# A spectral-filter and gated-MLP kernel: the first three gated units made one row tile at a time, seven units in the first pass, two projections at the end

## The chip, the cores and the metric

The kernel runs on one core of a Trainium2 chip. The metric is the device time of one execution in microseconds (us), as the median of several runs. The core has a matrix engine (PE, with its weight loads shown apart as PEld), a vector engine (DVE), a scalar engine (ACT), a general engine (POOL) and a queue that issues most DMAs (SP; ACT can issue DMAs too). Each engine takes its own instructions in program order and waits on semaphores for the others.

## The reference: what is computed

The input `x` has 2048 rows of 512 bf16 numbers. It is normalized by rows, and two branches are added to it:

```python
xn = _layernorm(x, axis=-1)
return x + _A_ref(xn, A_w_r, A_w_i) + _B_ref(xn, B_w_gate, B_w_up, B_w_down)

# branch A: a filter in the frequency domain, W = w_r + 1j * w_i
irfft2(rfft2(xn) * W)
# branch B: a gated MLP, 512 -> 1792 -> 512
h = gelu(xn @ w_gate) * (xn @ w_up)
h @ w_down
```

## The kernel before, in words

The 2048 rows are 16 row tiles of 128 rows (`NJ`), and four of them are a block of 512 rows (`b` from 0 to 3). The 1792 hidden columns are 14 chunks of 128 (`fc`).

**Branch B.** For a block, the normalized rows `xn` are transposed to `xnT` (four chunks of 128 of the 512 columns lie on the partitions). `geglu_unit(b, fc, a, w)` (L529) makes one chunk of the hidden layer for `w` rows from row `a` of the block: four gate matmuls into one PSUM bank, four up matmuls into the next (L543), a gelu of the gate bank on ACT into `gg` (L555), and a product of the up bank and `gg` on DVE into `hT` (L563). Its PSUM banks come from a ring; a bank is taken again when its reader (the gelu or the product) is done. Such a unit is called a gated unit here. `down_unit(b, jj)` (L577), a projection, makes one row tile of the output: 14 matmuls (L589) and an addition into `x_sb` on DVE (L600).

**Branch A** is a 2-D Fourier filter as small matmuls (L616, L642, L691, L722, L753, L774), with shuffles through DRAM between its stages: A and d for each row tile, then B, a product and c for each of 16 pairs, then e and fin for each row tile. The first stage needs the normalized rows folded: POOL makes half folds (L504) of four tiles at a time, DVE mirror folds (L509). `unit_fin` (L765) ends the branch for one row tile: ACT and DVE unpack the bank (L781, L784, L785), DVE and POOL make two halves (L788), POOL adds them into `x_sb` (L792). The later of this and the projection's addition issues the row tile's output DMA on SP (L575).

**The order is written out by hand** (L798 to L909). A recording layer keeps a list for each engine in the order in which the Python calls come, and puts a wait for every dependency that the engine has not waited for yet. So whatever stands earlier in a list holds back all that stands behind it on that engine. The order is:

1. Loads. ACT issues the identity and columns 0 to 383 of `w_up` (chunks 0 to 2); SP issues row tiles 0 and 1 of `x`, the same columns of `w_gate`, row tiles 2 and 3, then the other weight pieces and rows (L343 to L375). Each piece has one semaphore for both matrices.
2. Row tiles 0 and 1: statistics on DVE (`ln_stats`, L411 and L412), the root of both on ACT (L417), the reciprocal of both on DVE (L421), and the normalization of each on DVE (`ln_apply`, L434). Meanwhile PE runs 46 small warm-up matmuls on zeros, and 4 more that wait for the reciprocal (`NWARM`, L524). ACT loads the gelu's table and runs it once on one column (L802).
3. `transposes_by_tile(0, 2)` (L439): PE transposes both tiles into four banks (L447), one for each column chunk; DVE and ACT copy two banks each to `xnT` (L453, L455).
4. The statistics of tiles 2 and 3 on DVE, and their reciprocal root on POOL (`ln_rstd`, L426 and L427).
5. The first pass: block 0's gated units of chunks 0 to 5 (`NHALF` is 6) for the 256 rows of tiles 0 and 1, with a ring of six banks. After chunk 1 tiles 2 and 3 are normalized and POOL folds tiles 0 to 3; after chunk 3 tiles 2 and 3 are transposed (`transposes`, L473, copied at L480 and L482).
6. The same six units for tiles 2 and 3.
7. What is left of branch B is a list of fillers, in order: eight units of block 0, then units and projections of the later blocks (each block's four projections stand among the next block's units), and block 3's four projections at the end. Branch A's stages run one after another, and a filler is put between two of their steps: one filler before each A step (`j` from 0 to 15), some around the shuffles, one in each of 17 B and c steps (`u`), then all but 18 of those that are left, 15 between the e and fin steps, and the last 3 behind the last fin step. So a filler that is taken out of the list at its head moves all others one place forward.

Of the kernel before, what the change touches and what calls it, by code (L numbers as in the profile page):

```python
# [14 lines left out]
HD = 256  # L15
NK = 257
FF = 1792
P = 128
NJ = 16
NG = 32  # L20
NDC = 4
# [3 lines left out]
NWARM = (46, 4)  # L25
# [126 lines left out]
class _Sched:  # L152
# [14 lines left out]
    def total(self, stream):  # L167
        return (stream, self.stream_cnt[stream])
# [59 lines left out]
def bass_parallel_sum__spectral_gfnet__glu_gated_geglu__prompt_kernel(  # L228
# [21 lines left out]
    with ExitStack() as es:  # L250
# [68 lines left out]
        def sp_bank_bf(slot):  # L319
# [10 lines left out]
        streams = [("pe", 1), ("act", 1), ("dve", 1), ("pool", 1)]  # L330
        streams += [(n, 16) for n in ("x0", "x1", "x2", "x3", "xc1", "xc2", "xc3", "ident", "small", "fa", "eg", "wd", "wr", "wi",
                                      "w0", "w1", "w2", "w3", "w4", "dr0", "dr1", "perm1", "jx0", "jx1", "jx2", "jx3", "vd0_0", "vd0_1", "vd0_2", "vd1_0", "vd1_1", "vd1_2", "vd2_0", "vd2_1", "vd2_2", "vd3_0", "vd3_1", "vd3_2", "perm2", "tr2", "tr3", "out")]
# [106 lines left out]
        def transposes_by_tile(a, b, ring):  # L439

            n = (b - a) * P
            slots = [ring.alloc(1) for _ in range(NDC)]
            banks = [sp_bank_bf(slot)[:, 0:n] for slot, _ in slots]
            evs = []
            for j in range(a, b):
                for r in range(NDC):
                    ev_t = sch.op("pe", lambda e, j=j, r=r: e.transpose(banks[r][:, (j - a) * P:(j - a + 1) * P], xn[:, j, r * P:(r + 1) * P], ident),  # L447
                                  deps=[ev_id, ev_xn[j]] + slots[r][1])
                    if j < b - 1:
                        continue  # L450
                    dst = xnT[:, r, a * P:b * P]
                    if r % 2 == 0:
                        ev = sch.op("dve", lambda e, dst=dst, r=r: e.tensor_copy(dst, banks[r]), deps=[ev_t])  # L453
                    else:
                        ev = sch.op("act", lambda e, dst=dst, r=r: e.activation(dst, banks[r], ACT.Copy), deps=[ev_t])  # L455
# [73 lines left out]
        def geglu_unit(b, fc, a=0, w=512, ring=None):  # L529
# [6 lines left out]
            evw = [ev_w[i] for i, (lo, hi) in enumerate(WPIECES) if lo < (fc + 1) * P and fc * P < hi]  # L536
# [16 lines left out]
            ev_um = sch.op("pe", lambda e: mm(e, wu_sb, uslot), deps=udeps)  # L553
# [244 lines left out]
        NHALF = 6  # L798
        ln_stats(0)
        ln_stats(1)  # L800
        ev_sq = ln_sqrt(0, 2)
        sch.op("act", lambda e: e.activation(warm[:], eps_t[:], ACT.Gelu_apprx_tanh), deps=[ev_eps])  # L802
# [97 lines left out]
        filler(todo["left"] - 15 - 3)  # L900
# [59 lines left out]
```

## Time and profile before

| what | us |
|---|---|
| median of 3 runs | 180.47 (180.36 to 180.71) |
| profiled execution, its own time | 180.17 |
| its span in the trace | 178.4 |
| PE busy in the span | 174.7 |
| DVE busy | 116.0 |
| ACT busy | 86.5 |
| POOL busy | 55.2 |
| PE's first gated matmul starts | 7.14 |

The table is read so: the profiled execution is one run, 0.30 us under the median, and its span leaves out 1.8 us around the program. An engine's busy time is the sum of the time in which it has an instruction under way. In a timeline's line the first number is the start in us from the span's start, the second the time to the end of the last instruction of the group, then engine, source line, operation, what is written and read, shape and count; the bracket tells how long the engine was idle before and who ended it. PE's instructions overlap: the next starts before the one before has ended, so its pace is read from starts.

### The profile page before, as it was taken

What the parts mean: (1) busy time and instruction counts of PE and PEld (TensorE: products, weight loads), DVE (VectorE), ACT (ScalarE), POOL (GpSimd) and SP (SyncE); (2) the same over time, 40 slices, a digit from 0 to 9 for tenths busy, and PEclk for the clock granted to TensorE, in tenths of its full rate; (3) what the DMA queues carried; (4) which work ended last, traced back from release to release, by engine and by line L of the source; (5) the groups of instructions that cost most, each with busy time, mean ns of one, the idle gap of its engine ahead of it and who ended that gap; (6) DMA issues with size and microseconds to landing.
All of it is one profiled execution on the core that took longest, in us unless ns stands there. A gap on an engine that the chain in (4) does not pass through costs nothing.

```text
span 178.4 us, 3133 instructions
## 1 busy us (share of the span) xinstructions
PE 174.7 (98%) x1136; PEld 98.2 (55%) x1136; DVE 116.0 (65%) x250; ACT 86.5 (49%) x159; POOL 55.2 (31%) x54
## 2 busy tenths in 40 slices
PE   7999999999999999999999999999999999999994
PEld 7888465555555544454555555444455555555443
DVE  3768958798685628438586785954355868885731
ACT  2644357777362633066375764632173536662100
POOL 0073290373630000000000000000017869997760
PEclk9999999999999999999999999999999999999999
DMA  4999999999998693913435666744500111111101
GB/s 147 323 342 379 372 379 149 202 156 239 221 159 198 150 313 106 324 53 81 123 104 125 123 184 149 177 90 117 118 6 29 59 59 32 61 65 48 41 29 59
DMA packets 37520, 27.15 MB, mean 152 GB/s; under 512 B 6656, under 2 KB 36736, under 8 KB 37376
## 3 DMA queue, kind: packets, MB, share of 16 engines
q1 hardware_dynamic: 33664, 24.95, 55.1%
q10 hardware_dynamic: 3840, 2.00, 5.8%
q8 instruction: 9, 0.15, 0.4%
q14 instruction: 7, 0.06, 0.2%
HBM read 17.48 MB, written 6.30 MB: 133 GB/s over the span
## 4 chain that ended last, share of the span: by engine, by line
PE 87%; POOL 5%; DVE 5%; issue 1%
PE ps L543 48%; PE ps L589 25%; POOL bufC L504 5%; PE ps L524 3%; PE ps L722 2%; PE ps L753 2%; PE ps L774 2%; PE ps L691 2%; DVE bufA L434 2%; DVE hT L563 1%; PE ps L616 1%; PE ps L642 1%; PE ps L473 1%; DVE bufB L509 1%; POOL rstd L427 1%
## 5 line engine op out<-in xcount | busy, mean ns | idle before, releaser
L543 PE MATMUL ps<-xnT,wg_sb 128*128 128x512 bf16 (+1 forms) x248 | 58.5, 359 | 0.3 <-DVE xnT L453 0.3
L543 PE MATMUL ps<-xnT,wu_sb 128*128 128x512 bf16 (+1 forms) x248 | 58.6, 359 | 0.0
L563 DVE TENSOR_TENSOR hT<-ps,gg 128x512 bf16<-128x512 f32 (+1 forms) x62 | 39.3, 637 | 23.2 <-PE ps L543 21.6
L589 PE MATMUL ps<-wd_sb,hT 128*128 128x512 bf16 (+2 forms) x238 | 50.7, 367 | 0.0
L555 ACT ACTIVATE gg<-ps 128x512 bf16<-128x512 f32 (+1 forms) x62 | 34.4, 555 | 25.2 <-PE ps L543 23.6
L788 POOL TENSOR_TENSOR bufC<-bufC 128x256 bf16<-128x256 f32 x16 | 14.7, 919 | 86.5 <-DVE bufC L785 86.5
L543 PEld LDWEIGHTS ps<-xnT,wu_sb 128*128 128x128 bf16 x248 | 24.2, 98 | 24.2
L589 PEld LDWEIGHTS ps<-wd_sb,hT 128*128 128x128 bf16 x238 | 22.4, 98 | 23.2
L543 PEld LDWEIGHTS ps<-xnT,wg_sb 128*128 128x128 bf16 x248 | 23.0, 98 | 15.4 <-issue 0.5
L600 DVE TENSOR_TENSOR x_sb<-ps,x_sb 128x512 bf16<-128x512 f32 (+2 forms) x17 | 11.2, 660 | 23.9 <-PE ps L589 23.9
L792 POOL TENSOR_TENSOR x_sb<-x_sb,bufC 128x512 bf16<-128x512 bf16 x16 | 18.7, 1169 | 2.3
L504 POOL TENSOR_TENSOR bufC<-bufA 128x1024 bf16<-128x1024 bf16 x8 | 16.8, 2124 | 7.9 <-DVE bufA L434 7.9
L758 ACT ACTIVATE bufA<-ps 128x512 bf16<-128x512 f32 x16 | 9.4, 597 | 16.9 <-PE ps L753 16.9
L727 ACT ACTIVATE Vp<-ps 128x514 bf16<-128x514 f32 x16 | 9.5, 599 | 15.4 <-PE ps L722 15.4
L650 ACT ACTIVATE bufB<-ps 128x512 bf16<-128x512 f32 x16 | 11.9, 743 | 9.5 <-PE ps L642 9.5
L411 DVE BATCH_NORM_STATS2 st<-x_sb 128x6 f32<-128x512 bf16 x16 | 10.9, 678 | 2.2 <-DMA x_sb<-in_A_x_dram 2.2
L784 DVE TENSOR_TENSOR bufC<-bufC,ps 128x256 f32<-128x256 f32 x16 | 6.7, 421 | 5.3 <-ACT bufC L781 5.3
L696 ACT ACTIVATE Xc<-ps 128x514 bf16<-128x514 f32 x12 | 7.0, 595 | 1.0 <-PE ps L691 1.0
L623 ACT ACTIVATE tmp<-ps 128x512 bf16<-128x512 f32 x9 | 5.4, 597 | 4.4 <-PE ps L616 4.4
L426 POOL TENSOR_SCALAR rstd<-ag 128x4 f32<-128x4 f32 (+1 forms) x4 | 1.3, 316 | 19.9 <-DVE ag L412 19.9
L781 ACT ACTIVATE bufC<-ps 128x256 f32<-128x256 f32 x16 | 6.0, 378 | 2.6 <-PE ps L774 2.6
L788 DVE TENSOR_TENSOR bufC<-bufC 128x256 bf16<-128x256 f32 x16 | 6.8, 425 | 0.5
(50 smaller groups left out, 138.0 us busy)
## 6 DMA issues: line engine op xcount, KB each, us to landing
stage_g<-Vp SPq DMA_DIRECT2D x16, 128.5 KB, 3.1
bufC<-stage_p SPq DMA_DIRECT2D x4, 512.0 KB, 5.5
out_dram<-x_sb SPq DMA_DIRECT2D x15, 128.0 KB, 1.8
wd_sb<-in_B_w_down_dram SPq DMA_DIRECT2D x1, 1792.0 KB, 14.8
stage_p<-bufB SPq DMA_DIRECT2D x7, 256.0 KB, 5.6
wr_sb<-in_A_w_r_dram SPq DMA_DIRECT2D x6, 257.0 KB, 10.8
wi_sb<-in_A_w_i_dram SPq DMA_DIRECT2D x6, 257.0 KB, 10.0
JX<-Xc SPq DMA_DIRECT2D x24, 64.2 KB, 2.3
```

Of the source, the lines that this page charges most:

```text
L411: ev = sch.op("dve", lambda e: e.bn_stats(st[:, j, :], x_sb[:, j, :]), deps=[ev_x[j]])
L504: ev_hf[m] = [sch.op("pool", lambda e, t=t, op=op: e.tensor_tensor(half[:, m, t, :, :], rows[:, 0, :, :], rows[:, 1, :, :], op), deps=deps ...
L543: ins = e.matmul(gu_bank(slot)[:, 0:w], wsb[:, dc, fc * P:(fc + 1) * P], xnT[:, dc, b * 512 + a:b * 512 + a + w], start=(dc == 0), stop=(d ...
L555: ev_gg = sch.op("act", lambda e: e.activation(gg, gu_bank(gslot)[:, 0:w], ACT.Gelu_apprx_tanh), deps=[ev_gm] + gg_readers[s2])
L563: ev_h = sch.op("dve", lambda e: e.tensor_tensor(hT[hb][:, fc, a:a + w], gu_bank(uslot)[:, 0:w], gg, ALU.mult), deps=[ev_um, ev_gg] + hdeps)
L589: ins = e.matmul(bank(slot)[:, 0:w], hT[hb][:, fc, jj * P:(jj + 1) * P], wd_sb[:, fc, cs], start=(fc == 0), stop=(fc == NFC - 1))
L600: ev_a = sch.op("dve", lambda e, slot=slot, cs=cs, w=w: e.tensor_tensor(x_sb[:, j, cs], bank(slot)[:, 0:w], x_sb[:, j, cs], ALU.add), deps ...
L650: ev_T[j] = sch.op("act", lambda e: e.activation(dst, src, ACT.Copy), deps=[ev_p])
L727: ev_v = sch.op("act", lambda e: e.activation(Vp[sv][:], sp_pair(slot), ACT.Copy), deps=[ev_p] + Vp_readers[sv])
L758: ev_ZT[j] = sch.op("act", lambda e: e.activation(ZT[:, :, j, :], src, ACT.Copy), deps=[ev_p] + [ev_xnT[i][0] for i in (11, 15)])
L788: y = [sch.op(("dve", "pool")[h], lambda e, h=h, op=op: e.tensor_tensor(rS[s2][:, h * HD:(h + 1) * HD], yeS[s2][:, 0, :], yeS[s2][:, 1, :] ...
L792: ev_o = sch.op("pool", lambda e: e.tensor_tensor(x_sb[:, j, :], x_sb[:, j, :], rS[s2], ALU.add), deps=[a, b, ev_xn[j]] + ev_acc.get(j, []))
```

## The change

- **Loads.** SP issues row tiles 0 and 1, then columns 0 to 383 of `w_gate` and of `w_up`, then row tiles 2 and 3. ACT issues the identity alone. Gate and up pieces have semaphores of their own, and a unit's up matmuls wait for the up piece.
- **Tiles 0 and 1 apart.** The root is taken and inverted for each of the two tiles by itself. On DVE the order is: reciprocal 0, normalization 0, reciprocal 1, the two copies of tile 0's transposes, normalization 1. `transpose_first` transposes one tile into two banks of `ring_tr`, two column chunks in each, and copies them on DVE (tile 0) or ACT (tile 1). Tile 1's transposes stand behind tile 0's first unit.
- **Three units for one tile at a time.** Chunks 0 to 2 are made for the 128 rows of tile 0, then for those of tile 1. The statistics of tile 2 stand behind tile 0's units, those of tile 3 behind tile 1's first unit.
- **First pass of seven.** Chunks 3 to 6 follow for 256 rows; tiles 2 and 3 are normalized after chunk 3 and transposed after chunk 5. Then seven units for tiles 2 and 3. The list of fillers begins with seven units of block 0, so it is one shorter.
- **Warm-up** matmuls are 42 and 3, where they were 46 and 4.
- **The end.** 17 fillers are kept back for the e and fin steps and behind them, where it was 18: 15 as before, and 2 behind the last fin step.

```diff
@@ -22,7 +22,7 @@
 NFC = 14
 NGG = 3
 NX1 = 4
-NWARM = (46, 4)
+NWARM = (42, 3)
 LN_EPS = 1e-5
 
 
@@ -328,8 +328,9 @@
         ring_tr = _Ring((3, 4), bank_readers)
 
         streams = [("pe", 1), ("act", 1), ("dve", 1), ("pool", 1)]
+        streams += [("w%d%s" % (i, q), 16) for i in range(5) for q in "gu"]
 ...
-                                      "w0", "w1", "w2", "w3", "w4", "dr0", "dr1", ...)]
+                                      "dr0", "dr1", ...)]
         for name, inc in streams:
             sem = es.enter_context(nc.semaphore("sem_" + name))
             sch.add_stream(name, sem, inc)
@@ -349,8 +350,9 @@
             a, b = WPIECES[i]
             for q in which:
                 dst, src = ((wg_sb, B_w_gate), (wu_sb, B_w_up))[q]
-                load("w%d" % i, dst[:, :, a:b], src[:, a:b].rearrange("(r p) f -> p r f", p=P), eng=eng)
-            ev_w[i] = total("w%d" % i)
+                name = "w%d%s" % (i, "gu"[q])
+                load(name, dst[:, :, a:b], src[:, a:b].rearrange("(r p) f -> p r f", p=P), eng=eng)
+                ev_w[i, q] = total(name)
 
         def load_xc(m):
             ev = load("xc%d" % m, x_sb[:, 4 * m:4 * m + 4, :], xv[:, 4 * m:4 * m + 4, :])
@@ -358,11 +360,11 @@
                 ev_x[j] = ev
 
         ev_x = {}
-        load_w(0, (1,), eng="act")
-        for j in range(4):
+        for j in (0, 1):
             ev_x[j] = load("x%d" % j, x_sb[:, j, :], xv[:, j, :])
-            if j == 1:
-                load_w(0, (0,))
+        load_w(0)
+        for j in (2, 3):
+            ev_x[j] = load("x%d" % j, x_sb[:, j, :], xv[:, j, :])
         load_w(1)
         load_w(2)
         load_xc(1)
@@ -436,27 +438,28 @@
 
         ev_xnT = {}
 
-        def transposes_by_tile(a, b, ring):
-
-            n = (b - a) * P
-            slots = [ring.alloc(1) for _ in range(NDC)]
-            banks = [sp_bank_bf(slot)[:, 0:n] for slot, _ in slots]
+        def transpose_first(j, eng):
+
             evs = []
-            for j in range(a, b):
-                for r in range(NDC):
-                    ev_t = sch.op("pe", lambda e, j=j, r=r: e.transpose(banks[r][:, (j - a) * P:(j - a + 1) * P], xn[:, j, r * P:(r + 1) * P], ident),
-                                  deps=[ev_id, ev_xn[j]] + slots[r][1])
-                    if j < b - 1:
-                        continue
-                    dst = xnT[:, r, a * P:b * P]
-                    if r % 2 == 0:
-                        ev = sch.op("dve", lambda e, dst=dst, r=r: e.tensor_copy(dst, banks[r]), deps=[ev_t])
-                    else:
-                        ev = sch.op("act", lambda e, dst=dst, r=r: e.activation(dst, banks[r], ACT.Copy), deps=[ev_t])
-                    ring.add_reader(slots[r][0], ev)
-                    evs.append(ev)
-            for j in range(a, b):
-                ev_xnT[j] = evs
+            for h in range(2):
+                slot, bdeps = ring_tr.alloc(1)
+                bank = sp_bank_bf(slot)[:, 0:HD].rearrange("p (r s) -> p r s", r=2)
+
+                def f_tr(e, h=h, bank=bank):
+                    ins = None
+                    for r in range(2):
+                        ins = e.transpose(bank[:, r, :], xn[:, j, (2 * h + r) * P:(2 * h + r + 1) * P], ident)
+                    return ins
+
+                ev_t = sch.op("pe", f_tr, deps=[ev_id, ev_xn[j]] + bdeps)
+                dst, src = xnT[:, 2 * h:2 * h + 2, j * P:(j + 1) * P], bank
+                if eng == "dve":
+                    ev = sch.op("dve", lambda e, dst=dst, src=src: e.tensor_copy(dst, src), deps=[ev_t])
+                else:
+                    ev = sch.op("act", lambda e, dst=dst, src=src: e.activation(dst, src, ACT.Copy), deps=[ev_t])
+                ring_tr.add_reader(slot, ev)
+                evs += [ev, ev]
+            ev_xnT[j] = evs
 
         def transposes(a, b, ring, per=2):
 
@@ -533,7 +536,8 @@
             s2 = k % NGG
             hb = b % 2
             ring = ring or ring_gu
-            evw = [ev_w[i] for i, (lo, hi) in enumerate(WPIECES) if lo < (fc + 1) * P and fc * P < hi]
+            pieces = [i for i, (lo, hi) in enumerate(WPIECES) if lo < (fc + 1) * P and fc * P < hi]
+            evw, evw_up = ([ev_w[i, q] for i in pieces] for q in range(2))
             evx = [ev_xnT[4 * b + i] for i in range(a // P, (a + w) // P)]
             gslot, gdeps = ring.alloc(1)
 
@@ -550,7 +554,7 @@
             else:
                 ev_gm = sch.op("pe", lambda e: mm(e, wg_sb, gslot), deps=evw + evx + gdeps)
             uslot, udeps = ring.alloc(1)
-            ev_um = sch.op("pe", lambda e: mm(e, wu_sb, uslot), deps=udeps)
+            ev_um = sch.op("pe", lambda e: mm(e, wu_sb, uslot), deps=evw_up + udeps)
             gg = gg_sb[s2][:, 0:w]
             ev_gg = sch.op("act", lambda e: e.activation(gg, gu_bank(gslot)[:, 0:w], ACT.Gelu_apprx_tanh),
                            deps=[ev_gm] + gg_readers[s2])
@@ -795,27 +799,35 @@
             finished(j, ev_o)
 
 
-        NHALF = 6
+        NQUARTER, NHALF = 3, 7
         ln_stats(0)
         ln_stats(1)
-        ev_sq = ln_sqrt(0, 2)
+        ev_sq = [ln_sqrt(j, j + 1) for j in range(2)]
         sch.op("act", lambda e: e.activation(warm[:], eps_t[:], ACT.Gelu_apprx_tanh), deps=[ev_eps])
-        ln_recip(0, 2, ev_sq)
+        ln_recip(0, 1, ev_sq[0])
         for n, ev in zip(NWARM, (None, ev_rstd[0])):
             warm_up(n, ev)
         ln_apply(0)
+        ln_recip(1, 2, ev_sq[1])
+        transpose_first(0, "dve")
         ln_apply(1)
-        transposes_by_tile(0, 2, ring_sp)
+        for fc in range(NQUARTER):
+            geglu_unit(0, fc, 0, P, ring_first)
+            if fc == 0:
+                transpose_first(1, "act")
         ln_stats(2)
-        ln_stats(3)
+        for fc in range(NQUARTER):
+            geglu_unit(0, fc, P, P, ring_first)
+            if fc == 0:
+                ln_stats(3)
         ln_rstd(2, 4)
-        for fc in range(NHALF):
+        for fc in range(NQUARTER, NHALF):
             geglu_unit(0, fc, 0, 256, ring_first)
-            if fc == 1:
+            if fc == NQUARTER:
                 ln_apply(2)
                 ln_apply(3)
                 half_fold(0)
-            if fc == 3:
+            if fc == NHALF - 2:
                 transposes(2, 4, ring_tr)
         for fc in range(NHALF):
             geglu_unit(0, fc, 256, 256, ring_first)
@@ -897,7 +909,7 @@
                 back(u // 4 - 2, (u - 9) % 4, "act")
         for pq in range(2):
             back(3, pq, "sp")
-        filler(todo["left"] - 15 - 3)
+        filler(todo["left"] - 15 - 2)
         for j in range(NJ + 2):
             if j < NJ:
                 unit_e(j)
```

More of the change, by code (lines that the diff above doesn't have):

```diff
@@ L330, in bass_parallel_sum__spectral_gfnet__glu_gated_geglu__prompt_kernel @@
         streams = [("pe", 1), ("act", 1), ("dve", 1), ("pool", 1)]
+        streams += [("w%d%s" % (i, q), 16) for i in range(5) for q in "gu"]
         streams += [(n, 16) for n in ("x0", "x1", "x2", "x3", "xc1", "xc2", "xc3", "ident", "small", "fa", "eg", "wd", "wr", "wi",
-                                      "w0", "w1", "w2", "w3", "w4", "dr0", "dr1", "perm1", "jx0", "jx1", "jx2", "jx3", "vd0_0", "vd0_1", "vd0_2", "vd1_0", "vd1_1", "vd1_2", "vd2_0", "vd2_1", "vd2_2", "vd3_0", "vd3_1", "vd3_2", "perm2", "tr2", "tr3", "out")]
+                                      "dr0", "dr1", "perm1", "jx0", "jx1", "jx2", "jx3", "vd0_0", "vd0_1", "vd0_2", "vd1_0", "vd1_1", "vd1_2", "vd2_0", "vd2_1", "vd2_2", "vd3_0", "vd3_1", "vd3_2", "perm2", "tr2", "tr3", "out")]
         for name, inc in streams:
```

## The prediction

> **What bounds the kernel now.** I read the page first, then the timeline of the first 30 us, then the chain of waits and the timeline at the places where the chain leaves PE.
>
> ```profile
> span 178.4 us, 3133 instructions
> PE 174.7 (98%) x1136; PEld 98.2 (55%) x1136; DVE 116.0 (65%) x250; ACT 86.5 (49%) x159; POOL 55.2 (31%) x54
> PE 87%; POOL 5%; DVE 5%; issue 1%
> ```
>
> PE is never long without work. So the change can gain only in the head (before PE's first gated matmul), in small PE waits, and in the tail after PE's last matmul. The matmuls stay the same in sum: only their cut into columns changes.
>
> The head, from the timeline (start, time to the group's end, engine, line):
>
> ```profile
> 0.97 5.41 PE L524 MATMUL ps<-hT 128*128 128x128 bf16 x50 [0.97 <-DVE hT L405]
> ...
> 4.67 0.18 DVE L412 BATCH_NORM_AGGREGATE ag<-st 128x2 f32<-128x6 f32 x1
> ...
> 5.20 1.28 ACT L802 ACT_TABLE_LOAD   x1
> ...
> 5.42 0.73 DVE L434 TENSOR_SCALAR bufA<-x_sb,ag,rstd 128x512 bf16<-128x512 bf16 x2
> ...
> 6.22 0.61 PE L447 MATMUL ps<-small,bufA 128*128 128x128 bf16 x8
> ...
> 6.70 0.49 DVE L453 COPY xnT<-ps 128x256 bf16<-128x256 bf16 x2 [0.55 <-PE ps L447]
> 6.76 0.66 ACT L455 ACTIVATE xnT<-ps 128x256 bf16<-128x256 bf16 x2
> ...
> 7.14 0.62 PE L543 MATMUL ps<-xnT,wg_sb 128*128 128x256 bf16 x4 [0.31 <-DVE xnT L453]
> ...
> 7.93 0.66 DVE L411 BATCH_NORM_STATS2 st<-x_sb 128x6 f32<-128x512 bf16 x1
> ...
> 9.20 0.73 POOL L427 TENSOR_TENSOR rstd<-rstd,half_t 128x2 f32<-128x2 f32 x1
> ...
> 9.97 0.74 DVE L434 TENSOR_SCALAR bufA<-x_sb,ag,rstd 128x512 bf16<-128x512 bf16 x2 [0.39 <-POOL rstd L427]
> ...
> 10.76 0.62 PE L473 MATMUL ps<-small,bufA 128*128 128x128 bf16 x8
> ```
>
> To see: a matmul's end lies 0.2 to 0.3 after its slot, so 50 warm-ups in 5.41 are about 0.107 apart, the eight transposes 0.056 (0.61 less 0.22, by 7). Between the two, at about 6.1, the clock opened (the page's clock row doesn't show it, the pace does). PE then waits from about 6.67 to 7.14 for copies. And PE waits once more for DVE: the second transposes start at 10.76, 0.11 after the slot before them was due to end.
>
> **Prices.** Four matmuls of 256 columns start 0.437 apart (7.59 to 8.03), so 0.109 each; of 512, 0.216; of 128, 0.056. An operation not in this trace is the 128-column gelu: 256 columns take 0.38, 512 take 0.60, so 0.27 (between the 0.20 of the one-column gelu and 0.38); the product likewise 0.42 and 0.69, so 0.285 (0.18, an aggregate, to 0.42). Successive operations of DVE and ACT overlap by some 0.1 (two normalizations of 0.41 in 0.73). A handover costs 0.04 to DVE or ACT, 0.05 to 0.11 to PE.
>
> **The head, walked.** The statistics don't move: DVE's second aggregate still starts at 4.67. Root 0 is then done (tile 0's aggregate ends at 4.06, the root takes 0.30). Reciprocal 0 at 4.77, normalization 0 from 4.97 to 5.39, against 5.83. But PE holds 45 warm-ups in front: 0.97 + 45 x 0.1065 = 5.76. So tile 0's four transposes take 5.75 to 6.17, still at the slow pace; the pairs end at 6.17 and 6.33, DVE's copies at 6.50 and 6.70. First gate matmuls 6.64, the third and fourth at 6.76 and 6.82 behind copy two, up 6.87 to 7.09. **PE starts 0.50 earlier.**
>
> Normalization 1 now stands on DVE behind the two copies: 6.61 to 7.02, against 5.74 to 6.15. Tile 1's transposes take PE's slots 7.09 to 7.31, which before lay ahead of the units. ACT: gelu 0 at 7.11, the two copies of tile 1 at 7.40 and 7.68, and only then gelu 1 at 7.96 and gelu 2 at 8.23. PE: units 1 and 2 to 8.21 (eight matmuls each, 0.445), tile 1's three units to 9.54; its copies end at 8.07, in time. DVE: the products of units 1 and 2 at 8.3 and 8.55, and only behind them the statistics of tile 2 at 8.79, which before started at 7.11. From here I walk DVE: statistics to the next operation 0.80, product 0.20, statistics of tile 3 at 9.79, its aggregate ends at 10.66; from there to the normalizations 1.17 (before: 8.80 to 9.97, over POOL), which run from 11.83 to 12.57. PE: chunks 3, 4, 5 at 0.874 from 9.54, 0.06 lost to the bank of a late product, end 12.22. **The second transposes start at 12.62, so PE waits 0.39 there,** where it was 0.11. Eight transposes 0.445, chunk 6 0.874, 0.04 for the copies: the second half starts at 13.98, its seven units end at 20.09.
>
> Before, block 0's seventh chunk would end at 18.21 + 4 x 0.216 x 2 = 19.94. The head costs **+0.15**: PE starts 0.50 earlier, but 0.22 of transposes now stand behind that start, the 128-column cut costs 24 x (2 x 0.056 - 0.109) = 0.06 and chunk 6's cut 0.02, the first unit's gaps 0.07, and the wait for DVE is 0.28 longer. Ends: -0.25 if that wait doesn't come, +0.55 with rival B.
>
> Here the Trainium skill speaks against the change: "TensorE: Matmul & The Clock Gate", section "Back-to-back issue gap", gives some 81 ns for a 128-column weight-load and matmul pair in a stream. The trace's transposes are such pairs, at 56 ns. By the page the 48 would cost 48 x 0.081 - 24 x 0.109 = 1.3 us more, an estimate by that page; I take the trace.
>
> **DMAs.** `w_up`'s first piece leaves ACT's queue (0.54 of issue, nothing waits for it there) and goes to SP at 2.11. Its landing: the piece issued at 2.11 before took 4.7, so 6.8 by that; needed at 6.87. Cost 0; 0.3 if it is that late again. All later loads are issued one slot (0.43) later: the next pieces landed at 8.1 and 9.0 and are needed at 9.54 and 9.98. Cost 0. The added waits for up pieces are five, of 0.05 each on PE's sequencer, which runs ahead: 0 (at most 0.25).
>
> **Fillers one place forward.** All projections move one step earlier among branch A's steps. One PE wait hangs on that, seen in the chain of waits:
>
> ```profile
> 46.62 4.22 POOL bufC L504 x2
> ...
> 52.75 0.61 DVE bufB L509
> 53.36 0.04 issue
> 53.40 0.40 PE ps L616 x4
> ```
>
> PE's last up matmul before it was due to end at 53.16 (52.30 + 0.86): 0.24 lost, waiting for the mirror fold of tiles 12 to 15. The projections stand at steps 9 and 13 before, 8 and 12 after, so between the fold's start (step 8) and this A step PE gets 3.02 - 1.73 = 1.29 more work. The fold moves only 0.25 (its normalization stands behind the projection's addition). **-0.24** (0 if the wait reappears at another step).
>
> Against that: the cover between the last d step and the first B step shrinks by 1.29 (two projections and four units become one and five). The last shuffle lands 11.9 after that d step, PE arrives after 11.88: 0 to 0.1, and less because the queue of the first shuffle doesn't move; I take 0. In the B and c steps PE loses 0.13 and 0.10 at two c steps (82.78, 102.86), both behind a unit's product on DVE; after the shift ACT issues the returning DMAs (L739) beside gelus more often: **+0.05** (-0.1 to +0.2). The e steps' wait of 0.2 at 128.6 keeps its cover of four units and a projection: 0.
>
> **The tail.**
>
> ```profile
> 169.20 1.40 POOL L792 TENSOR_TENSOR x_sb<-x_sb,bufC 128x512 bf16<-128x512 bf16 x1
> ...
> 171.43 1.15 POOL L792 TENSOR_TENSOR x_sb<-x_sb,bufC 128x512 bf16<-128x512 bf16 x1
> ...
> 175.38 0.56 DVE L600 TENSOR_TENSOR x_sb<-ps,x_sb 128x384 bf16<-128x384 f32 x1 [1.58 <-PE ps L589]
> 176.17 0.29 DVE L600 TENSOR_TENSOR x_sb<-ps,x_sb 128x128 bf16<-128x128 f32 x1 [0.22 <-PE ps L589]
> ```
>
> With two projections behind the last fin step instead of three, POOL's last addition comes 3.02 later: 172.58 + 3.02 = 175.60. The addition at 175.38 waits for it, 0.25 late; the one that ends the kernel, at 176.17, waits for PE all the same, and only its DMA is issued 0.1 behind. **+0.05** (0 to 0.25).
>
> **The sum:** 0.15 - 0.24 + 0.05 + 0.05 = 0.01, on the profiled execution's 180.17. That run lies 0.30 below the median; put on the median, 180.47 + 0.01 = 180.5.
>
> **Rivals.** What can be told from no change here is 0.2%, 0.36 us: 180.1 to 180.8.
>
> A, faster (0.23): DVE reaches tiles 2 and 3 in time, because the 128-column operations cost nearer to their lower ends, and the second transposes don't wait. The 0.39 and 0.06 go, and the sum is -0.44: 180.0. For it: DVE is idle 0.5 before its first copies, and the stretch is short. Against it: two statistics, POOL's 1.17 and two normalizations stand in line behind unit 2's product.
>
> B, slower (0.25): the 128-column gelu and product cost what the 256-column ones do (0.38, 0.42). Gelu 2, and with it tile 2's statistics, come 0.27 later, tile 3's 0.41, and the second transposes start at 13.03: +0.42 in sum, 180.9. It decides from the point where tile 3's normalization ends later than 12.93. A late `w_up` piece moves the same line.
>
> C: the change starts no gated unit earlier because of PE's own warm-ups. Then 0.5 is lost more, 181.0; the walk has the warm-ups end at 5.76, so I give it no chance of its own; it is in B's.
>
> One more rule, by itself: the same page of the Trainium skill, section "Part 4: PE-mode transpose", says that transposes don't count as PE work for the clock gate. Tile 0's transposes now stand where the clock was about to open; no run here shows what that does.
>
> **Chances.** Forecast, within 0.2%: 0.52; A 0.23; B 0.25. The range takes in A's 180.0 and, over B's 180.9, half of the DMA and tail bounds: 180.0 to 181.1.
>
> **What would show it.** PE's first L543 at 6.6 and tile 2's L411 at 8.8 (right), PE's wait ahead of L473 at 0.3 to 0.5 (below 0.1: A; above 0.75: B), no gap ahead of L616 near 54, POOL's last L792 ending at 175.4 to 175.8 less the shift. The prediction is wrong if the clock opens elsewhere, or if another wait among the B, c and e steps takes over the 0.24.

## The result: 182.91 us, 1.3% slower, and the profile after

The changed kernel takes **182.91 us** (median of 4 runs, 182.63 to 182.96); the kernel before takes 180.53 beside it (180.36 to 180.71). The ratio is 1.0129, with a 95% interval of 1.0111 to 1.0146. Forecast was 180.5, in a range of 180.0 to 181.1: the time lies 1.8 above the range's end. The profiled execution took 182.96 us. The lines of its page that answer to those of before (span, busy time, chain of waits by engine):

```profile
span 181.2 us, 3209 instructions
PE 174.0 (96%) x1163; PEld 98.1 (54%) x1163; DVE 116.1 (64%) x255; ACT 87.4 (48%) x164; POOL 55.3 (31%) x54
PE 68%; POOL 13%; DMA 9%; DVE 3%; issue 3%; SPq 2%; POOLq 1%; ACT 1%; ACTq 0%; DVEq 0%
```

PE is no busier than before (174.0 against 174.7), so the 2.8 us of span are waits. In the chain PE's share fell from 87 to 68%; POOL's rose from 5 to 13%, and DMA has 9%. POOL and DMA are where to look.

**The head** is not the place. PE's timeline, matmuls alone (the line numbers are now three or four higher):

```profile
6.21 0.39 PE L547 MATMUL ps<-xnT,wg_sb 128*128 128x128 bf16 x4 [0.36 <-DVE xnT L457]
6.84 0.40 PE L547 MATMUL ps<-xnT,wu_sb 128*128 128x128 bf16 x4 [0.24 <-DMA wu_sb<-in_B_w_up_dram]
...
10.31 0.61 PE L547 MATMUL ps<-xnT,wu_sb 128*128 128x256 bf16 x4 [0.18 <-DMA wu_sb<-in_B_w_up_dram]
...
12.63 0.62 PE L476 MATMUL ps<-small,bufA 128*128 128x128 bf16 x8
...
20.14 0.81 PE L547 MATMUL ps<-xnT,wg_sb 128*128 128x512 bf16 x3
```

The last line is the first 512-column unit, chunk 7. Before, the same point of the work lies at 19.93: the head (what stands ahead of this point) costs 0.21. From there to the last c steps (pairs 14 and 15) PE gains: 0.24 ahead of the A step near 53, where the wait is gone as forecast, and 0.10 at a c step near 102. The last c steps start at 119.61, 0.16 ahead of the same point of the work before.

**In the middle** the changed kernel loses 1.24. The chain of waits in order of time (start, length, what), before and after, up to the first e step:

```profile
118.65 6.91 PE ps L543 x32
125.56 3.02 PE ps L589 x14
128.58 0.04 issue
128.63 0.62 PE ps L753 x8
```

```profile
121.14 5.28 DMA stage_g<-Vp
126.42 0.02 issue
126.43 0.33 SPq L743
126.76 0.04 issue
126.81 4.58 DMA bufB<-stage_g
131.38 0.04 issue
131.43 0.62 PE ps L757 x8
```

Before, the chain runs through PE: four units and a projection, then 0.2 of waiting. After, it runs through the last write of the c steps to DRAM (into `stage_g`, called the last write below) and the last return from it (into `bufB`, the last return); PE has done the same four units and projection by 129.98, and waits 1.45. The transfers are the same, but they took 5.28 and 4.58 us from issue to landing, where before they took 4.42 and 4.19: 0.86 + 0.39 = 1.25, which is the loss.

**The tail** loses 1.7: from PE's last matmul to the end of the span it is 3.95 after and 2.25 before. DVE's and POOL's timeline of the changed kernel:

```profile
163.38 1.16 POOL L796 TENSOR_TENSOR x_sb<-x_sb,bufC 128x512 bf16<-128x512 bf16 x1
...
164.64 0.69 DVE L604 TENSOR_TENSOR x_sb<-ps,x_sb 128x512 bf16<-128x512 f32 x1 [1.99 <-POOL x_sb L796]
165.24 0.41 DVE L788 TENSOR_TENSOR bufC<-bufC,ps 128x256 f32<-128x256 f32 x1
...
166.06 0.96 POOL L792 TENSOR_TENSOR bufC<-bufC 128x256 bf16<-128x256 f32 x1 [1.53 <-DVE bufC L789]
167.17 1.15 POOL L796 TENSOR_TENSOR x_sb<-x_sb,bufC 128x512 bf16<-128x512 bf16 x1
...
168.43 0.69 DVE L604 TENSOR_TENSOR x_sb<-ps,x_sb 128x512 bf16<-128x512 f32 x1 [1.98 <-POOL x_sb L796]
...
176.98 1.15 POOL L796 TENSOR_TENSOR x_sb<-x_sb,bufC 128x512 bf16<-128x512 bf16 x1
178.23 0.76 DVE L604 TENSOR_TENSOR x_sb<-ps,x_sb 128x384 bf16<-128x384 f32 x2 [1.29 <-POOL x_sb L796]
```

With two projections behind the last fin step instead of three, the projection of row tile 11 (then 12, 13) stands right behind the fin step of the same row tile. Its addition on DVE (L604) waits for POOL's addition of that row tile (L796). DVE stands still for 2.0 us; behind the addition in its list are the next fin step's unpackings (L788, L789), and POOL, idle 1.53, waits for those. It is a loop of DVE and POOL: from one L604 to the next 3.79 us, where PE needs 3.47 for a step. POOL's last addition ends at 178.13 instead of 172.58. In before's timeline the additions of the same row tiles waited for PE, 3.47 apart:

```profile
163.15 0.69 DVE L600 TENSOR_TENSOR x_sb<-ps,x_sb 128x512 bf16<-128x512 f32 x1 [1.13 <-PE ps L589]
...
165.11 0.96 POOL L788 TENSOR_TENSOR bufC<-bufC 128x256 bf16<-128x256 f32 x1 [1.21 <-DVE bufC L785]
...
166.62 0.69 DVE L600 TENSOR_TENSOR x_sb<-ps,x_sb 128x512 bf16<-128x512 f32 x1 [1.13 <-PE ps L589]
```

### The profile page after: what moved, and what is told of

Its sections match the earlier page's. It is cut to its first block, busy times and chain, and to the rows that moved or that the text cites. A ratio compares the mean times of both kernels' runs of the same rounds, so it can differ in the third digit from the quotient of the medians.

```text
span 181.2 us, 3209 instructions
## 1 busy us (share of the span) xinstructions
PE 174.0 (96%) x1163; PEld 98.1 (54%) x1163; DVE 116.1 (64%) x255; ACT 87.4 (48%) x164; POOL 55.3 (31%) x54
## 4 chain that ended last, share of the span: by engine, by line
PE 68%; POOL 13%; DMA 9%; DVE 3%; issue 3%; SPq 2%; POOLq 1%; ACT 1%; ACTq 0%; DVEq 0%
PE ps L547 41%; PE ps L593 17%; POOL x_sb L796 7%; POOL bufC L792 5%; DMA wu_sb<-in_B_w_up_dram 3%; DMA stage_g<-Vp 3%; DMA bufB<-stage_g 3%; PE ps L646 2%; PE ps L620 2%; PE ps L695 2%; PE ps L726 2%; SPq L340 2%; DVE bufC L789 1%; DVE bufC L788 1%; PE ps L757 1%
## 5 line engine op out<-in xcount | busy, mean ns | idle before, releaser
L547 PE MATMUL ps<-xnT,wu_sb 128*128 128x512 bf16 (+2 forms) x264 | 59.2, 347 | 0.4 <-DMA wu_sb<-in_B_w_up_dram 0.4
L547 PE MATMUL ps<-xnT,wg_sb 128*128 128x512 bf16 (+2 forms) x264 | 59.2, 347 | 0.4 <-DVE xnT L457 0.4
L567 DVE TENSOR_TENSOR hT<-ps,gg 128x512 bf16<-128x512 f32 (+2 forms) x66 | 39.5, 606 | 27.1 <-PE ps L547 25.3
L559 ACT ACTIVATE gg<-ps 128x512 bf16<-128x512 f32 (+2 forms) x66 | 35.1, 533 | 26.5 <-PE ps L547 22.7
L547 PEld LDWEIGHTS ps<-xnT,wu_sb 128*128 128x128 bf16 x264 | 24.9, 98 | 24.6 <-DMA wu_sb<-in_B_w_up_dram 0.9
L547 PEld LDWEIGHTS ps<-xnT,wg_sb 128*128 128x128 bf16 x264 | 23.8, 98 | 15.2 <-issue 0.7
L604 DVE TENSOR_TENSOR x_sb<-ps,x_sb 128x512 bf16<-128x512 f32 (+2 forms) x17 | 11.1, 660 | 24.3 <-PE ps L593 16.0
L796 POOL TENSOR_TENSOR x_sb<-x_sb,bufC 128x512 bf16<-128x512 bf16 x16 | 18.7, 1170 | 2.3
L788 DVE TENSOR_TENSOR bufC<-bufC,ps 128x256 f32<-128x256 f32 x16 | 6.7, 419 | 4.6 <-ACT bufC L785 4.6
L757 PEld LDWEIGHTS ps<-fa,bufB 128*128 128x128 bf16 x64 | 4.8, 98 | 5.1 <-DMA bufB<-stage_g 1.8
L757 PE MATMUL ps<-fa,bufB 128*128 128x128 bf16 x64 | 6.0, 219 | 1.3 <-DMA bufB<-stage_g 1.3
## 6 DMA issues: line engine op xcount, KB each, us to landing
stage_g<-Vp SPq DMA_DIRECT2D x16, 128.5 KB, 3.4
```

Of the source, the lines that this page charges most:

```text
L547: ins = e.matmul(gu_bank(slot)[:, 0:w], wsb[:, dc, fc * P:(fc + 1) * P], xnT[:, dc, b * 512 + a:b * 512 + a + w], start=(dc == 0), stop=(d ...
L559: ev_gg = sch.op("act", lambda e: e.activation(gg, gu_bank(gslot)[:, 0:w], ACT.Gelu_apprx_tanh), deps=[ev_gm] + gg_readers[s2])
L567: ev_h = sch.op("dve", lambda e: e.tensor_tensor(hT[hb][:, fc, a:a + w], gu_bank(uslot)[:, 0:w], gg, ALU.mult), deps=[ev_um, ev_gg] + hdeps)
L604: ev_a = sch.op("dve", lambda e, slot=slot, cs=cs, w=w: e.tensor_tensor(x_sb[:, j, cs], bank(slot)[:, 0:w], x_sb[:, j, cs], ALU.add), deps ...
L757: ins = e.matmul(sp_bank(slot)[:, ci * P:(ci + 1) * P], V[:, j, V0[ci]:V0[ci] + HD - 1:2], EM[:, j, :], start=True, stop=True)
L796: ev_o = sch.op("pool", lambda e: e.tensor_tensor(x_sb[:, j, :], x_sb[:, j, :], rS[s2], ALU.add), deps=[a, b, ev_xn[j]] + ev_acc.get(j, []))
```

## The experiments

Three theories at first: **L** (the shifted list and the shorter end lose the time), **H** (the head does), and for L its two places: **T** (the loop of DVE and POOL in the tail) and a late return from DRAM, with **Q** (ACT issues it behind gelus) and **K** (other fillers stand beside it) as reasons. Each time is a median; each ratio stands against the kernel before on the same chip. "Old head" and "new head" are the head of the kernel before and of the changed one. The cover of a transfer is the PE work that stands beside it.

### e1: the list alone, on the kernel before

```diff
-        NHALF = 6
+        NHALF = 7
-        filler(todo["left"] - 15 - 3)
+        filler(todo["left"] - 15 - 2)
```

> The kernel before with its own head, but a first pass of seven units and two projections behind the last fin step, so that all fillers stand one place forward. Theory L (the shifted fillers cost the time, at two places: PE's wait ahead of the first e step grows from 0.2 to 1.4 us, and at the end each projection's addition on DVE waits for POOL): 182.4 to 183.0 us, both signs there. Rival H (the new head costs it, by its one-tile units, load order or clock): 180.1 to 180.5 us.

182.30 us, ratio 1.0109 (1.0077 to 1.0141). L holds: with the old head most of the loss is there. But it is not spent in the same place. The first e step waits 0 here; PE's wait sits between two c steps, for DVE:

```profile
119.83 0.39 PE L722 MATMUL ps<-tmp,small 128*128 128x257 bf16 x2
120.65 0.40 PE L722 MATMUL ps<-tmp,small 128*128 128x257 bf16 x2 [0.43 <-DVE tmp L710]
```

### e2 to e4: an earlier return, and later additions, on the changed kernel

e2 issues one of the returns on ACT one step earlier:

```diff
-            if u in (9, 10, 13, 14, 17, 18):
-                back(u // 4 - 2, (u - 9) % 4, "act")
+            if u in (9, 10, 13, 14, 16, 18):
+                back(u // 4 - 2, {16: 0}.get(u, (u - 9) % 4), "act")
```

> The changed kernel with one DMA issue moved: the first returning DMA of the third part is issued on ACT a step earlier, ahead of the c step's copy and the unit's gelu. Theory Q (that issue waits behind the gelu on ACT, so its traffic meets the last staged writes and delays the last return): the wait ahead of the first e step falls from 1.45 to 0.2 to 0.5 us, time 181.7 to 182.0 us. Rival R (the last writes and the last return take that long whatever else is under way): wait and time unchanged, 182.7 to 183.0 us.

183.00 us, ratio 1.0144 (1.0109 to 1.0179). The return was issued at 116.8 instead of 118.95, and the wait ahead of the first e step is 1.47: Q is refuted.

e3 takes the additions of row tiles 11 to 13 out of the loop, behind the next fin step's work on DVE (called "late" below):

```diff
-                ev_a = sch.op("dve", ...)
-                ring.add_reader(slot, ev_a)
-                finished(j, ev_a, cs, h == 0)
+                def add(slot=slot, cs=cs, w=w, h=h, ev_dn=ev_dn, ring=ring):
+                    ev_a = sch.op("dve", ...)
+                    ring.add_reader(slot, ev_a)
+                    finished(j, ev_a, cs, h == 0)
+                if j in (11, 12, 13):
+                    late.append(add)
+                else:
+                    add()
...
                 unit_fin(j - 2)
+                while late:
+                    late.pop(0)()
```

> The changed kernel, with the projections' additions of row tiles 11, 12 and 13 put on DVE behind the next fin step's DVE work; PE's and POOL's orders are untouched. Theory T (an addition that waits for POOL's addition of the same row tile holds up the next fin step's work on DVE, which POOL waits for in turn): steps at the end fall back from 3.8 to 3.5 us, POOL's last addition ends 1.4 to 1.7 us earlier, time 181.1 to 181.5 us. Rival P (POOL's own two operations a step set the end): 182.6 us or more.

181.55 us, ratio 1.0058 (1.0038 to 1.0078), 1.36 less than the changed kernel (1.3 by the two ratios). Its timeline, DVE and POOL:

```profile
164.95 0.42 DVE L795 TENSOR_TENSOR bufC<-bufC,ps 128x256 f32<-128x256 f32 x1 [2.26 <-ACT bufC L792]
...
166.08 0.68 DVE L605 TENSOR_TENSOR x_sb<-ps,x_sb 128x512 bf16<-128x512 f32 x1
...
168.42 0.42 DVE L795 TENSOR_TENSOR bufC<-bufC,ps 128x256 f32<-128x256 f32 x1 [1.66 <-ACT bufC L792]
...
175.50 1.15 POOL L803 TENSOR_TENSOR x_sb<-x_sb,bufC 128x512 bf16<-128x512 bf16 x1
```

The addition (L605 here) no longer waits, DVE waits for PE's pace through ACT instead, and a step is 3.47 again (164.95 to 168.42). T is shown.

The edits of e2 and e3 together (e4):

> The changed kernel with both edits (the early return and the later additions). If the two places are independent and are all of the loss, the gains add: 180.0 to 180.5 us. If one hides the other, 181 us or more. If the new head has a cost of its own beyond the 0.2 us that the trace shows, 180.8 us or more.

181.38 us, ratio 1.0055 (1.0038 to 1.0071). Not the sum that was expected of independent gains: the earlier return adds nothing that can be told apart.

### e5 and e6: the projections of block 2 one place later

So that a projection is the filler of step `u` = 17 again, the last c step that has a filler, as before:

```diff
-                    units.insert(at + n, ("d", b - 1, n))
+                    units.insert(at + n + (b == 2), ("d", b - 1, n))
```

> The changed kernel, with block 2's projections one place later among its units, so that one stands again in the last c step that has a filler, as before. Theory K (the wait ahead of the first e step is the 3.0 us projection that was replaced there by a 1.7 us unit: the staged writes and returns of the last c steps take the same time, and 1.3 us less PE work lies beside them): wait back from 1.45 to 0.1 to 0.5 us, time 181.6 to 182.0 us. Rival J (these DMAs take longer by themselves in the changed kernel): wait 0.9 us or more, time 182.5 us or more.

182.74 us, ratio 1.0110 (1.0080 to 1.0139). The wait ahead of the first e step fell from 1.45 to 0.93, not to K's 0.1 to 0.5, and the time is J's. The last write took 4.33 instead of 5.28, the last return 5.00 instead of 4.58 (the chain of waits):

```profile
121.28 4.33 DMA stage_g<-Vp
...
126.00 5.00 DMA bufB<-stage_g
```

So K is right at most in part: another filler there does not bring the return back to 4.2.

With "late" as well (e6):

> The changed kernel with block 2's projections one place later and the additions of row tiles 11 to 13 behind the next fin step's DVE work. If theories K and T are both right and are all of the loss: 180.2 to 180.6 us. If only T is right: 181.2 to 181.6 us, with a wait of 0.9 us or more ahead of the first e step.

181.19 us, ratio 1.0021 (1.0000 to 1.0042); a wait of 1.22 is left ahead of the first e step.

### e7 and e8: the same with the old head, and the end alone

e7 is the kernel before with the two edits of e1, block 2's projections one place later, and "late":

> The kernel before with its own head and a first pass of seven units, two projections behind the last fin step, and the two repairs of the run before it in this list. Against that run it differs by the head alone. The walk in the prediction gives the new head a cost of 0.15 us, the traces 0.2 to 0.5 us with a late w_up piece: this one 0.1 to 0.5 us faster, 179.9 to 180.4 us. Rival: the new head gains, and this one is slower by 0.2 us or more.

180.65 us, ratio 0.9992 (0.9975 to 1.0009). The new head costs some 0.54 here (against e6, same chip), more than the 0.21 of the first 20 us. The last return took 4.17 us and PE's wait was 0.54. But single executions can't price a head to 0.2: the start of chunk 7 lies at 19.93 to 20.66 in the profiled executions of the seven kernels with the old head, and at 20.12 to 20.70 in those of nine with the new one (e15 apart).

e8 is the kernel before with the end alone, so six fillers stand ahead of the e steps and two behind:

```diff
-        filler(todo["left"] - 15 - 3)
+        filler(todo["left"] - 15 - 2)
```

> The kernel before, where only 17 instead of 18 fillers are kept for the e and fin steps: six instead of five run ahead of the first e step, and two projections instead of three behind the last fin step. Theory T (each projection's addition now meets its own row tile's addition on POOL): 1.5 to 1.7 us lost at the end, 0.2 us gained as the wait ahead of the first e step goes: 181.6 to 182.0 us. Rival: without the longer list the end costs nothing, 180.2 to 180.4 us.

181.81 us, ratio 1.0055 (1.0028 to 1.0082). One number in one line, and the loop of DVE and POOL is there:

```profile
163.43 0.69 DVE L600 TENSOR_TENSOR x_sb<-ps,x_sb 128x512 bf16<-128x512 f32 x1 [1.98 <-POOL x_sb L792]
164.86 0.96 POOL L788 TENSOR_TENSOR bufC<-bufC 128x256 bf16<-128x256 f32 x1 [1.53 <-DVE bufC L785]
...
175.78 1.15 POOL L792 TENSOR_TENSOR x_sb<-x_sb,bufC 128x512 bf16<-128x512 bf16 x1
```

### e9 and e10: one more filler as cover

On e6 (e9) and on e7 (e10), taken from behind the third e step:

```diff
-        filler(todo["left"] - 15 - 2)
+        filler(todo["left"] - 14 - 2)
...
-            if 1 <= j < NJ:
+            if 1 <= j < NJ and j != 2:
                 filler()
```

> The changed kernel with block 2's projections one place later and the additions of row tiles 11 to 13 put back (as in e6), and one more filler ahead of the e steps, six instead of five, taken from behind the third e step. If all that is left of the loss in the middle is that PE has done its fillers before the last return from DRAM lands (1.2 us in e6), the filler's 1.73 us covers it: no wait ahead of the first e step, and some 180.0, which is e6's 181.19 less 1.2. If the return only moves with whatever is put in front of it, or the wait comes back among the e steps, 181 or more.

180.24 us, ratio 0.9970 (0.9955 to 0.9985).

> The same on the kernel before with the shifted list: its head, seven units in the first pass, block 2's projections one place later, additions put back, six fillers ahead of the e steps. e7's wait there was 0.5: 180.1 if it goes. Against e9 this gives the new head's own price once more: 0.2 by the traces' first 20 us (e9 slower than this one by 0.2), or 0.5 and more if the new head also costs something that doesn't hang on the wait ahead of the e steps.

180.00 us, ratio 0.9962 (0.9946 to 0.9978). Neither has a wait ahead of the first e step. e6's timeline and then e10's show the two cases:

```profile
129.10 1.03 PE L547 MATMUL ps<-xnT,wu_sb 128*128 128x512 bf16 x4
131.18 0.62 PE L764 MATMUL ps<-fa,bufB 128*128 128x128 bf16 x8 [1.06 <-DMA bufB<-stage_g]
```

```profile
130.95 1.03 PE L543 MATMUL ps<-xnT,wu_sb 128*128 128x512 bf16 x4
131.81 0.61 PE L760 MATMUL ps<-fa,bufB 128*128 128x128 bf16 x8
```

In e10 the up matmuls are followed by the e step after 0.86, their own pace. So what is left of the loss in the middle is an uncovered transfer, and a filler's 1.73 us covers it: by the ratios 0.9 came back with the new head (e6 to e9) and 0.5 with the old one (e7 to e10), where PE's waits had been 1.22 and 0.54. The new head's price, with the transfer covered, is 0.24 (e9 less e10).

### e11 to e14: why the last return is longer

e11 is e6 with the first piece of `w_up` on ACT's queue again:

```diff
+        load_w(0, (1,), eng="act")
         for j in (0, 1):
             ev_x[j] = load("x%d" % j, x_sb[:, j, :], xv[:, j, :])
-        load_w(0)
+        load_w(0, (0,))
```

> e6 with one thing undone: the first piece of w_up is issued by ACT again, first of all loads, and not by SP behind w_gate. In all six kernels with the new loads the last return from DRAM took 4.6 to 5.0 us from issue to landing, in three of the four with the old loads 4.2. If the queue that the load stands in sets this (each later transfer of SP then finds another place), the last return takes 4.2 here, the wait ahead of the first e step falls from 1.2 to some 0.6, and the time to some 180.6. If it is chance, or the rest of the head, 4.6 to 5.0 and 181.2.

181.36 us, ratio 1.0034 (1.0015 to 1.0054).

e12 is e7 the other way round:

```diff
-        load_w(0, (1,), eng="act")
...
-                load_w(0, (0,))
+                load_w(0)
```

> The other way round: e7 (the old head, shifted list, block 2's projections one place later, additions put back) with the first piece of w_up moved from ACT to SP, behind w_gate. If the load's queue sets the length of the last return: 4.6 to 5.0 instead of 4.17, a wait of some 1.0 to 1.3 ahead of the first e step, 181.2 or more with the head's own cost. If not: 4.2, a wait of 0.5, and 180.65, or up to 0.4 more if the units wait for w_up's landing.

180.74 us, ratio 0.9999 (0.9974 to 1.0024). The load's queue is not the reason, in either direction. Then the semaphores, given to the old head (e13, on e7) and taken from the new one (e14, on e6, the same lines the other way round):

```diff
-                load("w%d" % i, ...)
-            ev_w[i] = total("w%d" % i)
+                name = "w%d%s" % (i, "gu"[q])
+                load(name, ...)
+                ev_w[i, q] = total(name)
...
-            ev_um = sch.op("pe", lambda e: mm(e, wu_sb, uslot), deps=udeps)
+            ev_um = sch.op("pe", lambda e: mm(e, wu_sb, uslot), deps=evw_up + udeps)
```

> e7 (the old head, shifted list, block 2's projections one place later, additions put back) with the gate and up pieces on semaphores of their own and the up matmuls waiting for theirs; all else as in e7. If the semaphores make the last return from DRAM slow, it takes 4.6 to 5.0 us here instead of 4.2, PE waits 1.0 to 1.3 ahead of the first e step, and the time is 181.1 to 181.3. If not: 4.2, a wait of some 0.5, and e7's 180.65.

> e6 (the new head, block 2's projections one place later, additions put back) with one semaphore for a gate piece and its up piece again. The first gate matmul then waits for w_up's landing as well, some 0.5 at the head at most. If the semaphores make the last return slow, it takes 4.2 here and the wait ahead of the first e step falls from 1.2 to some 0.5: 180.6, or up to 181.0 with the later start. If not: 4.6 to 5.0, and 181.2 to 181.6.

180.57 us, ratio 0.9983 (0.9958 to 1.0008), and 182.29 us, ratio 1.0091 (1.0061 to 1.0121). They aren't the reason either. e14 is slower than expected: its first gate matmul waits for `w_up` too, but its runs lie 2.3 us apart (181.16 to 183.49), and the profiled one is the fastest of them, so what the slow ones wait for isn't seen.

From issue to landing in us, one profiled execution each, and PE's wait ahead of the first e step:

| kernel | head | last write | last return | PE's wait |
|---|---|---|---|---|
| before | old | 4.42 | 4.19 | 0.21 |
| e7 | old | 4.77 | 4.17 | 0.54 |
| e12, `w_up` on SP | old | 4.55 | 4.10 | 0.24 |
| e13, semaphores | old | 4.47 | 4.15 | 0.19 |
| e10, more cover | old | 4.46 | 4.24 | 0 |
| after | new | 5.28 | 4.58 | 1.45 |
| e6 | new | 4.76 | 4.87 | 1.22 |
| e11, `w_up` on ACT | new | 4.90 | 4.78 | 1.28 |
| e14, one semaphore | new | 4.31 | 4.77 | 0.68 |
| e9, more cover | new | 4.73 | 4.66 | 0 |

The return took 4.10 to 4.24 in six of the seven kernels with the old head (e1 4.66), and 4.44 to 5.00 in all ten with the new one. **Why should a head that ends at 20 us lengthen a transfer at 127 us?** Not by its load's queue, not by its semaphores. The DMA view from 127 to 131.5 shows a candidate that no run tried alone. The changed kernel, then e7 (GB/s in 40 slices of the window, then queue and kind, packets, MB, share):

```profile
GB/s 0 146 0 18 73 91 50 64 132 159 264 328 337 337 328 337 273 219 205 209 200 187 178 155 141 118 100 59 23 14 18 14 14 14 5 0 0 0 0 0
q1 hardware_dynamic: 1056, 0.52, 57.9%
q8 instruction: 1, 0.02, 1.5%
```

```profile
GB/s 0 0 0 18 109 114 91 73 105 196 287 300 360 332 341 342 291 237 214 214 200 205 191 159 114 87 55 23 5 0 0 0 0 0 0 0 0 0 0 0
q1 hardware_dynamic: 1056, 0.52, 54.8%
```

The changed kernel's transfer ends in a tail of some 14 GB/s that e7's has not, and beside it ran one 16 KB packet of a queue of the kind "instruction" (from 127.15, for 1.06 us). All 17 traces fit this. The last return and the one just ahead of it run together. In nine kernels with the new head such a packet was under way among theirs, in e1 one of 8 KB: the last return took 4.58 to 5.00. In six with the old head none was: 4.10 to 4.24. In e15 it was over at 127.23, just after theirs began; there the issue of the last return took 1.19 (0.49 to 0.59 in the others), and the return 4.44. This packet, q8's seventh, starts in every kernel when PE has begun 1675 to 1704 of its matmuls and weight loads; the new head has 19 more of each than e7's, so it starts at 126.3 to 128.5 instead of 131.1 to 132.4. So the head may well reach the return through this packet, but that is a pairing, not an experiment: no run moved the packet alone. It doesn't settle the last write, whose lengths overlap (3.8 to 4.8 with the old head, 4.3 to 5.3 with the new one).

### e15: the new head mended

e9, with `w_up` on ACT as in e11 and tile 2's statistics ahead of tile 0's units:

```diff
         ln_apply(1)
+        ln_stats(2)
         for fc in range(NQUARTER):
             geglu_unit(0, fc, 0, P, ring_first)
...
-        ln_stats(2)
```

> e9 (the new head with all that was mended behind it) with the first piece of w_up issued by ACT again and tile 2's statistics on DVE ahead of tile 0's products instead of behind them. The 0.4 that PE waits ahead of the second transposes should go, since the two statistics then reach the normalizations 0.8 earlier: e9's 180.24 less 0.4, 179.8. If DVE is late for another reason (the products, 0.8 later, hold up the banks of the ring) nothing is gained: 180.2 or more.

**179.76 us**, ratio 0.9943 (0.9924 to 0.9963): it beats both kernels. PE's timeline, the second transposes and then chunk 7:

```profile
12.21 0.61 PE L477 MATMUL ps<-small,bufA 128*128 128x128 bf16 x8
...
19.71 1.03 PE L548 MATMUL ps<-xnT,wg_sb 128*128 128x512 bf16 x4
```

The transposes follow the matmuls ahead of them at once (11.78 + 0.44); in e11, with `w_up` on ACT alone, PE still waited 0.39 there, so the statistics did it. The first 512-column unit starts at 19.71, against 19.93 before, and ahead of all the other kernels: in this execution the head gains 0.22. The medians don't show that gain clear of noise: against e10, the best with the old head, the intervals overlap (0.9924 to 0.9963, 0.9946 to 0.9978).

## Why the prediction was wrong, point by point

- **"PE is never long without work", and three places to look:** right for before, and the three places are where the kernel lost. **The sum failed in two terms: the wait ahead of the first e step, put at 0, and the tail, put at +0.05.** They cost 1.24 and 1.7.
- **The head, +0.15:** 0.21 measured, in one pair of executions. The second transposes were forecast at 12.62 and came at 12.63; tile 2's statistics at 8.79 and came at 8.76; the up matmuls at 6.87 and came at 6.84. The first gate matmul came at 6.21 instead of 6.64, since the granted clock rose to full at 4.02 in this execution and at 6.14 in before's; the up matmuls' wait for `w_up` then gave that back. "The next pieces landed at 8.1 and 9.0. Cost 0" was wrong: `w_up`'s second piece landed at 10.27 and PE waited 0.34. It cost nothing more, because DVE would have held up the second transposes until 12.63 all the same (the wait there was 0.12 instead of 0.39). e15 shows the term that made the head a loss, the statistics behind the products, as the walk said. The walk's bound for a late first piece of `w_up` was needed too: in the six other kernels in which SP loads it and the up matmuls alone wait for it, these start at 6.83 to 7.41, and where they start later the head ends later by as much. (The cut's 24 x (2 x 0.056 - 0.109) is 0.07, not 0.06.) That the clock opened elsewhere, a sign of being wrong by the prediction, is not what failed.
- **Rivals A and B:** neither came. The 128-column gelu took 0.28 (0.27 forecast), the product 0.27 to 0.29 (0.285).
- **The 128-column units:** eight matmuls in 0.445, as forecast, 0.055 to 0.056 each. The 81 ns of the Trainium skill's "TensorE: Matmul & The Clock Gate", section "Back-to-back issue gap", by which they would have cost 1.3 more (an estimate by that page), don't show here. What its section "Part 4: PE-mode transpose" says wasn't put to the test: the clock had opened 1.4 us ahead of the first transposes.
- **Fillers one place forward, -0.24:** right, the wait near 53 is gone. The B and c steps gained 0.10, where +0.05 was forecast.
- **"The e steps' wait of 0.2 at 128.6 keeps its cover of four units and a projection: 0":** failed, +1.24. The cover was kept exactly. But a wait of 0.2 means that the transfer behind it had no slack left, and the step took the transfer's length as fixed. The last write and the last return were 1.25 longer together. Rivals should have priced that: the profile before showed the same kind of write at 2.96 to 4.86 us between 109 and 120, and returns at 3.51 to 4.58; by the longest of each the term would have been 0.8. Why the two were longer stays open: for the return's 0.39 there is the candidate above, for the write's 0.86 none.
- **The tail, "+0.05 (0 to 0.25)":** failed, +1.7. The step put POOL's last addition 3.02 later, at 175.60, by moving it with PE's steps; it ended at 178.13. It looked at what the last addition waits for, and not at which addition stands ahead of which fin step's work in DVE's list. The order set a loop of DVE and POOL of 3.79 a step. e8 shows it (the end alone, 1.2 slower than before on the same chip, 181.81 against 180.62), and e3 (1.3 back by three additions issued later).
- **The sum:** 0.21 - 0.24 - 0.10 + 1.24 + 1.7 = 2.8 of span, as measured (181.2 less 178.4). From the changed kernel back, in ratios to before: 1.0129 as made, 1.0058 without the loop (e3), 1.0021 with block 2's projections back (e6), 0.9970 with the transfer covered (e9), 0.9943 with the head mended (e15). Seven units in the first pass and two projections at the end were no bad idea (e10, with both and the old head, is at 0.9962); they left two dependences without cover.

## What to carry to other kernels

Where a list of fillers is moved by one place, write down for each engine which instruction now stands ahead of which, and above all look for two engines that add into the same tile in turn: one that waits holds back what the other needs, and the loop sets a pace of its own. A wait of 0.2 us behind a DMA is a sign that its cover is used up, so price the DMA by the range that its kind shows in the profile, not by its one length (here 0.8 instead of 0, where 1.24 came). A change can be sound in its aim and lose by an order that one line mends, so take its parts one at a time before it is dropped.

## What was not expected of the hardware

- The same write and return through DRAM, with the same bytes and hardly another order, took 8.5 to 9.9 us together from one kernel to another (e1 3.83 + 4.66, e5 4.33 + 5.00, the changed kernel 5.28 + 4.58).
- Kernels whose profile shows PE waiting for that return spread more from run to run: e11 1.5 us in 10 runs, e14 2.3 in 10, e6 1.0 in 10; with the transfer covered e9 0.46 and e10 0.52, in 12 runs each. That the transfer makes the spread is argued, not shown: the changed kernel's four runs lie within 0.33, while e13, whose wait is 0.19, spreads 1.4 in 10, and the kernel before, with 0.21, spread 2.1 in 20 runs beside it.
- The granted clock rose to full at 3.75 to 6.14 us from kernel to kernel (where warm-ups run then, they go from 0.107 to 0.056 apart), PE being busy from 0.97 in all. The order of the head doesn't set it, in the 13 traces that record it: old heads 3.81, 5.06, 5.13, 5.51, 5.51, 6.14; new ones 3.75, 3.77, 4.02, 4.63, 4.86, 5.38, 5.60.
- One 16 KB packet of an instruction queue beside a return of 256 KB goes with 4.6 to 5.0 us instead of 4.1 to 4.2, as told above. That it is the cause isn't shown.
